# Fused two-part kernel on one core: attention's paired steps joined, transfers planned longer, all orders rewritten

## The chip, the cores and the metric

The kernel runs on one core of one Trainium2 chip. The metric is the device time of one execution in microseconds (us). A core has five engines that matter here, each with its own queue of instructions that it works through strictly in order: TensorE (PE in the profile; PEld is its weight load), VectorE (DVE), ScalarE (ACT), GpSimd (POOL) and SyncE (SP). SP computes nothing; it issues transfers (DMAs) between the core's memory and DRAM. GpSimd issues transfers too.

## What is computed

All data is float32. The first part is a two-way attention for 8 batches and 8 heads, with 512 tokens and 32 state rows of 64 features:

```python
scores = scale * np.matmul(x, state.transpose(0, 1, 3, 2))     # tokens against states
a = np.exp(scores - scores.max(-1, keepdims=True))
a /= a.sum(-1, keepdims=True) + 1e-09
xread = np.matmul(a, state)
scores2 = scale * np.matmul(state, x.transpose(0, 1, 3, 2))    # states against tokens
a2 = np.exp(scores2 - scores2.max(-1, keepdims=True))
a2 /= a2.sum(-1, keepdims=True) + 1e-09
sread = np.matmul(a2, x)
out = np.concatenate([xread, sread], axis=2)
```

The second part takes the 8 x 544 = 4352 rows of 512 features that come out of it through two dense layers of 2048 hidden features:

```python
h = x @ w_in
sp = np.maximum(h, 0.0) + np.log1p(np.exp(-np.abs(h)))   # softplus
g = h * erf(sp)
return g @ w_out
```

## The kernel before

**The algebra.** The product of attention weights, states and `w_in` is regrouped: `mixed` multiplies a batch's states by `w_in` ("M"), and `first_product` multiplies M by the transposed attention weights `aT`, so that `xread` is never formed. The large products are done with seven block products in place of eight (Strassen and Winograd forms; `seven`, `second_product`, and twice over in `twice_product`), which is why there are many additions of blocks on VectorE (`sums_y`, `sums_a`, `sums_w`, the L848 sums of M).

**Stages.** Batch 0 is done in a way of its own during the load of the weights (`begin0`, `mixed0`, `first0`, `serf0`, `second0`). Weights come in through `fetch_in`, `fetch_out` and `fetch_pair` and are rebuilt on ScalarE and VectorE by `convert` (L549 to L557). Then come batches 1 to 7 with the first half of the hidden features (the rounds), each a `unit`: `sums_a`, `second_product` or `twice_product`, with the next batch's `mixed` and `first_product`, and the attention (`attend`) of the batch after that, worked in between. Then the state rows (`first_states`, `second_states`), and then all batches again with the second half of the hidden features.

**The attention of one batch** (`attend`, from L676). Two halves `e` of 512 columns each hold four heads apiece. Per half, in order: four transposes of the x tiles on VectorE (L685; four tiles in all), the scores on TensorE (L693), a copy out of PSUM by ScalarE (L699) into `sc`, then on VectorE a 32 x 32 block transpose into `xT` (L715), the maximum over states (L718), the subtraction (L721), the maximum over tokens (L724) and its scaling (L727), on ScalarE the exponentials (L730 for the token side, L734 for the state side, with the sums accumulated), and on VectorE the sums (L742), the reciprocals (L120 and L121, once for the token side and once for the state side), the scaling (L747), the transpose into `aT` (L752) and the transpose of the state side's weights (L758). Each of the steps stands in a `for e in range(2)` loop, one instruction for each half. At the end `send` writes `xT` to DRAM (`kept_t`, L763) and `receive` reads it back in another layout (L768). `xT` is one buffer for all batches: the next batch's L715 overwrites what L763 reads. The result `sread` is scaled into `sn` by VectorE (L805) in `read`.

**Softplus, erf and the product** (`serf`): ScalarE does softplus (L958) and erf (L973), VectorE the multiplication (L976), then the sums of `sums_a` (L987); TensorE's second product (L1020) reads what these write. Softplus, erf and exp need different function tables, and a change of table is an instruction of its own (ACT_TABLE_LOAD).

**What sets the order.** Every piece of work is recorded by `op(engine, cost, at, go, reads, writes, ...)` with a planned cost. The order on each engine is written out by hand as a list of numbers (`ORDER`, five lists). `emit` walks the five lists with the planned costs, adds a planned cost where ScalarE's table changes, holds transfers back by a planned occupation (`pipe`) and a planned landing (`land`), and emits the instructions in the order of planned begin; `in_order` then pins each engine to that order. So costs set the merge of the engines' lists, but on one engine the order is that of the list. `BY_VECTOR` names the copies out of PSUM that VectorE does; the others go to ScalarE (`either`). `spare_products` are products of an identity matrix that fill waits of TensorE in the first 25 us or so (L115); their results are not used.

Of the kernel before, what the change touches and what calls it, by code (L numbers as in the profile page):

```python
# [11 lines left out]
ALU = mybir.AluOpType  # L12
ACTF = mybir.ActivationFunctionType
AX = mybir.AxisListType
# [3 lines left out]
def kernel(  # L18
# [17 lines left out]
    nc = tc.nc  # L36
# [103 lines left out]
    def op(engine, cost, at, go, reads=(), writes=(), table=None, land=0.0, pipe=0.0):  # L140
# [14 lines left out]
        x0 x2 s00 ta1 m000 m011 m020 m021 m120 m121""".split())  # L155

    def either(name, cost, out, in_, at, reads, writes):

        if name in BY_VECTOR:
            op(DVE, cost[1], at, lambda: nc.vector.tensor_copy(out(), in_()), reads, writes)  # L160
        else:
            op(ACT, cost[0], at, lambda: nc.scalar.copy(out(), in_()), reads, writes)
# [3 lines left out]
            0-1 5 2-3 6 4 8-9 7 15 22-23 17 16 12 24-25 18 10-11 19 13-14 20 26-30 21 34 33 45 31-32  # L166
            54 46 53 47 56 55 71 35 62 37 36 38 48 39-41 70 49 63 57-58 66 74 59-60 43 42 51-52 50
            73 69 44 77-79 61 65 93 81-82 80 83 64 86 84-85 72 76 88-89 94 90 87 95 75 91-92 67 102
            96 68 103 106 97 107 98-99 104 108 130 109 105 132-133 131 137 110 134 111-113 135
            114-115 136 118 140 116 139 138 117 141 119 122-123 143 142 124 100 144 125 101 120-121  # L170
            145 147 126-127 177 128-129 179-180 178 184 181 149-151 182-183 152 186-187 157 153
            158-159 154 160-161 165 188 185 166 189 162-163 167 191 146 155 164 156 148 190 169 168
            170-171 194 192 172 196-198 224 199 173 225-227 174 204 231 228 175 205 229 176 200 234
            206 201 233 230 235 207 202 208 203 232 236 209 237 210-211 238 193 212 195 213-214 239
            241 215 271 243 216 274 217-219 244 273 220 245 272 240 275 221 278 276 242 246 222-223
            281 251-252 277 247 253 248-249 282 280 279 254 250 283 255 284 256-259 286 285 263-265
            260 319 288 287 290 318 291 266 292 261-262 320 293 321 267-268 322 294-295 289 296 325
            269-270 323-324 302 298 328 297 303-306 329 327 326 330 299-301 331 310 307 311 308
            312-313 309 333 332 334 314 364 315 336 316-317 366 365 367 338 337 368 371 343 339 335
            369 344-346 370 340 373-374 347 406 375 372 348-349 376-377 341-342 357 350 359 358 407  # L180
            361 360 352 351 354 353 362-363 356 410-411 355 385 408 387 386 388 378 389 409 390 380
            391 379 382 381 412-413 383-384 414-415 399 392 416-417 393-394 418-419 395 400 396 402
            436 434-435 401 397 403 398 440 420-421 441 437 442-443 404 438-439 444-445 405 446-447
            422-423 449 448 428-429 424 464 425 465 426 432-433 467 427 466 468 430-431 469 471 470
            452 474 454 472 475 455 473 477 476 453 479 478 460 458 450 508 451 456 459 457 509 511
            510 462 461 463 512 487 480 515 489 488 490-491 513 482 481 483 518 492 514 517 484 519
            516 493 485 521 520 501 486 503 494 522-523 496 552 495 502 504 497-498 555 505 499
            553-554 507 506 556 531 500 533 532 559 534-535 524 557-558 525-526 561 528 527 562
            536-537 529 563 560 545 564-565 547 566-567 530 546 538 549 548 539-540 596 542 541 599
            543 550 598 551 603 575 597 544 600 577 568 601 576 578 569 602 579 570 606 572 571 604  # L190
            581 605 607 574 573 580 608-609 582 589 611 610 590-591 640 584 583 585 642 593 592 586
            641 643 595 587 644 619 588 594 645 620-621 612 647 622 614 646 650 623 616 613 615 649
            625 651 648 624 652 617-618 633 653 626 654-655 628 627 635 634 637 636 629-630 684 638
            685 687 686 632 688 639 631 663 689 656 691 657-658 690 693 665 694 664 667 692 666 668
            660 695 659 661 696-697 662 669 699 698 670 677 672 671 729 679 673 678 681 728 674 682
            680 676 731 683 675 707 730 708 710 732 709 700 733 735 711 734 738 702 737 713 739 736
            704 712 701 703 741 705 721 740 706 723 722 714 743 742 725 724 716 715 772 718 774 773
            717 719 775 727 779 776 720 751 726 777-778 753 744 752 754 745 755 746 780 782 748 783
            756 747 784-785 757 749 781 765 750 766 758 768 760 759 767 762 761 769 764 763 770 786
            771 787-790 793 791 795 792 794 797 800 796 802 801 803-804 799 798 807 806 805 809 808  # L200
            814 811 810 816 812 815 818 817 813 819-820""",
        ACT: """
# [1511 lines left out]
```

## Time and profile before

| what | value |
|---|---|
| three runs | 703.06, 703.60, 704.51 us; median 703.6 |
| the profiled execution | 703.79 us, of which the profile's span is 702.0 us |
| granted TensorE clock | 0.999 of full speed |
| busy: PE, PEld, DVE, ACT, POOL | 692.0, 583.9, 593.1, 471.8, 85.6 us |
| moved by DMA | 92.88 MB, mean 132 GB/s |

Times in the trace count from the start of the span. A row of the timeline gives the start, the duration, the engine, the line of the program (L715 is line 715), the operation, what it writes and reads, the shape, the count, and in square brackets the idle time of the engine just before it and what ended that. Instructions of one engine overlap a little at their ends, so the distance between two starts is what a row of instructions really costs. Matmuls are pipelined and their ends are modelled.

### The profile page before, as it was taken

What the parts mean: (1) busy time and instruction counts of PE and PEld (TensorE: products, weight loads), DVE (VectorE), ACT (ScalarE), POOL (GpSimd) and SP (SyncE); (2) the same over time, 40 slices, a digit from 0 to 9 for tenths busy, and PEclk for the clock granted to TensorE, in tenths of its full rate; (3) what the DMA queues carried; (4) which work ended last, traced back from release to release, by engine and by line L of the source; (5) the groups of instructions that cost most, each with busy time, mean ns of one, the idle gap of its engine ahead of it and who ended that gap; (6) DMA issues with size and microseconds to landing.
All of it is one profiled execution on the core that took longest, in us unless ns stands there. A gap on an engine that the chain in (4) does not pass through costs nothing.

```text
span 702.0 us, 13245 instructions
## 1 busy us (share of the span) xinstructions
PE 692.0 (99%) x5193; PEld 583.9 (83%) x5193; DVE 593.1 (84%) x989; ACT 471.8 (67%) x849; POOL 85.6 (12%) x93
## 2 busy tenths in 40 slices
PE   9999999999999999999999999999999999999997
PEld 7534778687878878899999879898989898989997
DVE  6999999899999999896954589686859697869797
ACT  6997997949778475947264665848386748585732
POOL 0001011001010010000100100202043222222231
PEclk9999999999999999999999999999999999999999
DMA  8858896965968655311654502516085536415376
GB/s 284 205 147 201 187 230 168 292 156 174 202 230 189 161 206 188 95 62 30 168 178 180 144 1 83 98 16 114 1 143 68 106 38 114 54 22 70 60 112 116
DMA packets 133742, 92.88 MB, mean 132 GB/s; under 512 B 93744, under 2 KB 120752, under 8 KB 133168
## 3 DMA queue, kind: packets, MB, share of 16 engines
q1 hardware_dynamic: 114336, 61.88, 31.9%
q0 software_dynamic: 18800, 29.63, 23.0%
q8 instruction: 41, 0.67, 0.4%
q10 hardware_dynamic: 544, 0.52, 0.2%
q14 instruction: 21, 0.17, 0.1%
HBM read 50.86 MB, written 41.16 MB: 131 GB/s over the span
## 4 chain that ended last, share of the span: by engine, by line
PE 81%; DVE 9%; ACT 2%; issue 1%; DVEq 0%; ACTq 0%
PE o L1256 30%; PE h L936 17%; PE o L1020 15%; PE at L936 7%; PE o L1439 4%; PE h L1390 2%; PE at L837 2%; PE h L837 2%; PE at L799 1%; DVE ring L976 1%; PE at L1390 1%; DVE ring L987 1%; PE h L693 1%; DVE xT L721 1%; DVE xT L715 1%
## 5 line engine op out<-in xcount | busy, mean ns | idle before, releaser
L948 ACT COPY ring<-h 128x512 f32<-128x512 f32 x120 | 69.1, 584 | 80.4 <-PE h L936 75.0
L976 DVE TENSOR_TENSOR ring<-ring 128x1024 f32<-128x1024 f32 (+1 forms) x64 | 73.0, 1152 | 26.6 <-ACT ring L973 26.2
L936 PE MATMUL h<-aT,m 128*128 128x256 f32 x360 | 92.2, 382 | 0.2 <-ACT ring L948 0.2
L1020 PE MATMUL o<-w_out,ring 128*128 128x256 f32 x320 | 77.7, 382 | 2.2 <-DVE ring L976 2.2
L958 ACT ACTIVATE ring<-ring 128x512 f32<-128x512 f32 x120 | 71.6, 629 | 8.5 <-DVE ring L950 5.5
L936 PEld LDWEIGHTS h<-aT,m 128*128 128x128 f32 x360 | 65.0, 190 | 11.1 <-ACT ring L948 1.1
L987 DVE TENSOR_TENSOR ring<-ring 128x1024 f32<-128x1024 f32 x60 | 72.8, 1220 | 0.4
L1020 PEld LDWEIGHTS o<-w_out,ring 128*128 128x128 f32 x320 | 59.9, 190 | 16.0 <-DVE ring L976 4.2
L1256 PE MATMUL o<-w_out,w_in 128*128 128x128 f32 x512 | 69.8, 276 | 0.0
L1256 PEld LDWEIGHTS o<-w_out,w_in 128*128 128x128 f32 x512 | 65.1, 192 | 3.5 <-issue 0.8
L1256 PE MATMUL o<-w_out,ring 128*128 128x128 f32 x480 | 64.6, 275 | 0.0
L973 ACT ACTIVATE ring<-ring 128x1024 f32<-128x1024 f32 (+1 forms) x64 | 63.4, 1008 | 0.2
L1256 PEld LDWEIGHTS o<-w_out,ring 128*128 128x128 f32 x480 | 60.0, 192 | 1.0 <-DVE ring L1281 0.2
L1020 PE MATMUL o<-raw,ring 128*128 128x256 f32 x240 | 58.6, 381 | 0.0
L1020 PEld LDWEIGHTS o<-raw,ring 128*128 128x128 f32 x240 | 44.9, 190 | 8.3 <-issue 1.7
L1256 PE MATMUL o<-raw,ring 128*128 128x128 f32 x360 | 48.7, 276 | 0.0
L1256 PEld LDWEIGHTS o<-raw,ring 128*128 128x128 f32 x360 | 45.3, 192 | 1.6 <-DVE xT L1238 0.8
L1176 POOL DMA_DIRECT2D out_dram<-oo x16 | 23.3, 1487 | 168.6 <-DVE ring L976 71.5
L1256 PE MATMUL o<-raw,xT 128*128 128x128 f32 x320 | 41.2, 276 | 0.1
L1256 PEld LDWEIGHTS o<-raw,xT 128*128 128x128 f32 x320 | 38.8, 192 | 2.6 <-ACT o L1287 0.8
L936 PE MATMUL h<-sy,m 128*128 128x256 f32 x120 | 30.9, 380 | 0.1
L936 PE MATMUL at<-sy,sx 128*128 128x256 f32 x120 | 31.0, 381 | 0.0
(269 smaller groups left out, 1400.5 us busy)
## 6 DMA issues: line engine op xcount, KB each, us to landing
x<-in_x_dram SPq DMA_DIRECT2D x30, 256.0 KB, 5.2
xq<-in_x_dram SPq DMA_DIRECT2D x112, 64.0 KB, 2.6
out_dram<-oo SPq DMA_DIRECT2D x10, 512.0 KB, 4.6
raw<-in_moe_w_in_dram SPq DMA_DIRECT2D x8, 512.0 KB, 6.9
raw<-in_moe_w_out_dram SPq DMA_DIRECT2D x4, 1024.0 KB, 5.7
raw<-in_moe_w_in_dram POOLq DMA_DIRECT2D x8, 512.0 KB, 5.7
raw<-in_moe_w_out_dram POOLq DMA_DIRECT2D x8, 512.0 KB, 5.6
kept_a<-aT SPq DMA_DIRECT2D x8, 512.0 KB, 4.2
```

The costliest lines, as they stand in the source:

```text
L837: nc.tensor.matmul(out=bank(names[k])[Ns * p:Ns * p + Ns, :], lhsT=st[r, b, q], rhs=of_group[2 * u + j][r, :, i, :], start=True, stop=True)
L936: nc.tensor.matmul(out=out_[:, i], lhsT=x_[:, q:q + P], rhs=y_, start=(start and i == 0), stop=(i == 1), skip_group_check=not start)
L948: op(ACT, 0.5, t, lambda: nc.scalar.copy(out_(), view(bank(name))), [name], w)
L958: op(ACT, 0.53, t, lambda: nc.scalar.activation(out=part(splane, k), in_=part(hplane, k), func=ACTF.Softplus), area(hplane, ks=[k], os=[o] ...
L973: op(ACT, 0.085 + 0.875 * share, at + n, lambda s_=s_: nc.scalar.activation(out=s_, in_=s_, func=ACTF.Erf), [], area(splane, ks=[k], os=os ...
L976: op(DVE, 0.065 + 1.075 * share, at + n + 1, lambda s_=s_, h_=h_: tt(s_, s_, h_, op=ALU.mult), area(hplane, ks=[k], os=os), area(splane, k ...
L987: op(DVE, 1.14, at + k, lambda k=k, x_=x_, y_=y_, how=how: tt(get("h", k), get(*x_), get(*y_), op=how), area(v[x_[0]], ks=[x_[1]]) + area( ...
L1020: nc.tensor.matmul(out=view(name)[:, h], lhsT=lhs[:, i, :], rhs=weight_of[n]()[:, u, i, :], start=(start and h == 0 and i == 0), stop=(h = ...
L1176: op(GP, 1.2, t, lambda: nc.gpsimd.dma_start(out=quad(r, c), in_=one(v), accum_op=ALU.add), every(*v), [("out", b, r, c)], land=3.0, pipe=2.0)
L1256: nc.tensor.matmul(out=out_[:, Q2 * k:Q2 * k + Q2], lhsT=lhs[:, k, i], rhs=rhs[:, i], start=first, stop=(k == len(ns) - 1 and i == 1), ski ...
L1390: nc.tensor.matmul(out=bank(bk)[:, P * i:P * i + P], lhsT=x_[:, i, k], rhs=y_[:, k], start=(start and i == 0 and k == 0), stop=(i == GF - ...
L1439: nc.tensor.matmul(out=bank("o%d" % bk)[:, E2 * c:E2 * c + E2], lhsT=ring[:, w_[w], plane, k][:, i, :], rhs=weight_of[n]()[:, u, i, :], st ...
```

## The change

1. In `attend`, the loops over the two halves become single instructions over 1024 columns: the transposes L715, L752 and L758, the maxima L718 and L724, the subtraction L721, the exponentials L730, the sums L742 and the scaling L747. The x transposes L685 go from four to two, except for batch 1, whose tiles arrive one by one. The two reciprocals (token and state side) become one, on one buffer `z`. The state side's exponential L734 stays in two.
2. The scaling into `sn` may now be done by ScalarE: `either` gets a `by` argument, and 5 of the 14 stay with VectorE. `BY_VECTOR` is rewritten, so other copies of batch 0's stage change engine.
3. Planned costs: a table load 1.28 becomes 1.41; occupations of transfers grow (x 5.2 to 6.0, `keep_y` 2.7 to 3.0, `put` 1.5 to 1.7, the late weight fetches 1.7 to 2.0, `kept_in` 0.9 to 1.2, batch 0's output 0.8 to 1.0).
4. All five lists of `ORDER` are new.

```diff
     BY_VECTOR = set("""
-        x0 x2 s00 ta1 m000 m011 m020 m021 m120 m121""".split())
+        x1 st s01 ta0 ta1 z1 m020 m021 u0 u1 m120 m121 sn11 sn40 sn41 sn51 sn70""".split())
...
+            if by:
+                nc.vector.tensor_scalar(out(), in_(), by(), None, op0=ALU.mult)
...
+            if by:
+                nc.scalar.activation(out=out(), in_=in_(), func=ACTF.Copy, scale=by())
...
-                cost, loaded[ACT] = cost + 1.28, table
+                cost, loaded[ACT] = cost + 1.41, table
...
-            op(SP, 3.0, 60, lambda: load_x_static(1), [], ["x"], land=4.0, pipe=5.2)
+            op(SP, 3.0, 60, lambda: load_x_static(1), [], ["x"], land=4.0, pipe=6.0)
...
-        for e in range(2):
-            dve(0.62, lambda e=e: nc.vector.transpose(out=both()[:, e], in_=sc()[:, e]),
-                [sc_of(b, e)], ["xT%d" % e])
-        for e in range(2):
-            dve(0.6, lambda e=e: nc.vector.reduce_max(out=m1()[:, e], in_=a(e), axis=AX.X),
-                ["xT%d" % e], ["m1%d" % e])
...
+        dve(1.19, lambda: nc.vector.transpose(out=flat(both()[:, 0:2]), in_=flat(sc())), scs, xts)
+        dve(1.136, lambda: nc.vector.reduce_max(out=m1(), in_=a(), axis=AX.X), xts, ["m1"])
+        dve(1.135, lambda: tt(a(), a(), over(m1()), op=ALU.subtract), ["m1"], xts)
+        dve(1.136, lambda: nc.vector.reduce_max(out=m2(), in_=sc(), axis=AX.X), scs, ["m2"])
...
+        op(ACT, 0.96, at + 6, lambda: nc.scalar.activation(
+            out=a(), in_=a(), func=ACTF.Exp, scale=scale), [], xts, table="exp")
...
-        dve(0.72, lambda: (inverse(z1()), inverse(z2())), [],
+        dve(0.37, lambda: inverse(z()), [],
...
-            op(DVE, 0.2, at + 1, lambda e=e: nc.vector.tensor_scalar(
-                sn_tile(b)[:, e], bank("at1")[:, D * e:D * e + D], d["z2"]()[:, e:e + 1], None,
-                op0=ALU.mult), ["at1", "z2%d%d" % (b % 2, e)], ["sn%d%d" % (b % 2, e)])
+            either("sn%d%d" % (b, e), (0.25, 0.2), lambda e=e: sn_tile(b)[:, e],
+                   lambda e=e: bank("at1")[:, D * e:D * e + D], at + 1,
+                   ["at1", "z2%d%d" % (b % 2, e)], ["sn%d%d" % (b % 2, e)],
+                   by=lambda e=e: d["z2"]()[:, e:e + 1])
```

The built program shows what the new lists do. VectorE has 900 instructions in place of 989, ScalarE 833 in place of 835, with 51 table loads in place of 53; TensorE has the same work, spare products included. On SP, in the list before, two pairs of `kept_a` and `kept_y` (`keep_y`) directly follow the third store of `xT` (L763); in the new list none stands between the third and the fourth store: batch 0's pair comes earlier, ahead of the x tiles of batch 2, and batch 3's after the fourth store. On VectorE, the work between the transpose L758 of one batch and the transpose L715 of the next is different in each round.

More of the change, by code (lines that the diff above doesn't have):

```diff
@@ L159, in either @@
         if name in BY_VECTOR:
[L160 removed]
+            op(DVE, cost[1], at, vector, reads, writes)
         else:
[L162 removed]
+            op(ACT, cost[0], at, scalar, reads, writes)
     ORDER = {
         PE: """
[L166 to L167 removed]
@@ L168 @@
[L168 to L173, printed above, removed]
```

306 lines of the change are left out of this document (151 added, 155 removed), and 4 rows, old and new, of the table ORDER.

## Prediction

> **What bounds the kernel now.** I read the page first.
>
> ```profile
> span 702.0 us, 13245 instructions
> PE 692.0 (99%) x5193; PEld 583.9 (83%) x5193; DVE 593.1 (84%) x989; ACT 471.8 (67%) x849; POOL 85.6 (12%) x93
> ```
>
> TensorE is busy for 692.0 of 702.0 us, and the change takes no matrix product away. So nothing that VectorE or ScalarE saves counts by itself; only TensorE's idle time can shrink, 10.0 us in all. The view of busy time by stretches says where it lies.
>
> ```profile
> 0.00:10.00 10.00, 8.94 (x115) 7.62 (x116) 3.45 (x6) 4.28 (x7) 0.69 (x6) 1.00 0.82 267
> 10.00:20.00 10.00, 9.16 (x101) 7.96 (x99) 9.60 (x21) 8.44 (x15) 0.00 (x0) 1.00 0.95 296
> 20.00:30.00 10.00, 9.82 (x49) 4.88 (x48) 9.93 (x15) 9.91 (x14) 0.00 (x0) 1.00 0.67 138
> 30.00:40.00 10.00, 9.57 (x42) 4.05 (x41) 9.15 (x14) 9.31 (x13) 0.00 (x0) 1.00 1.05 295
> 40.00:50.00 10.00, 9.85 (x51) 3.58 (x50) 9.72 (x15) 9.90 (x12) 0.00 (x0) 1.00 0.34 110
> 50.00:60.00 10.00, 9.94 (x29) 4.51 (x29) 9.97 (x17) 8.55 (x14) 0.93 (x2) 1.00 0.61 99
> 130.00:140.00 10.00, 8.66 (x40) 7.02 (x38) 7.29 (x14) 9.97 (x16) 0.01 (x1) 1.00 1.05 347
> 140.00:160.00 20.00, 19.06 (x87) 16.49 (x88) 19.93 (x29) 9.98 (x19) 2.89 (x5) 1.00 0.69 162
> 160.00:320.00 160.00, 160.00 (x1196) 132.22 (x1195) 151.29 (x262) 112.76 (x188) 6.86 (x12) 1.00 0.58 163
> 360.00:600.00 240.00, 240.00 (x1804) 215.60 (x1804) 180.44 (x293) 155.51 (x297) 39.18 (x34) 1.00 0.42 84
> 600.00:702.00 102.00, 97.25 (x772) 91.74 (x770) 83.93 (x142) 54.66 (x119) 23.00 (x20) 0.99 0.48 73
> ```
>
> The first figure after each stretch is its length; then come the busy times of TensorE, its weight loads, VectorE, ScalarE and GpSimd, the granted clock, the DMA engines' busy share and GB/s. Three places hold the idle time: the first 60 us (1.06 + 0.84 + 0.18 + 0.43 + 0.15 + 0.06 = 2.72), 130 to 160 us (1.34 + 0.94 = 2.28), and the end (4.75, the last results on their way out, which the change leaves as they are). From 160 to 320 and from 360 to 600 us there is none: savings there are worth nothing. In the first 60 us more is hidden, because spare products fill waits:
>
> ```profile
> L115 PE MATMUL o<-ident 128*128 128x128 f32 x64 | 8.4, 280 | 0.1
> ```
>
> These 8.4 us are no work, so an earlier start of real work could gain up to their length too. The waits of TensorE name one large one:
>
> ```profile
> PE o L1020 <- DVE ring L976: 2.2, 1, 2.2
> ```
>
> I looked at its neighbourhood in the timeline.
>
> ```profile
> 130.73 0.71 DVE L758 STREAM_TRANSPOSE xT<-xT 128x512 f32<-128x512 f32 x1
> 131.47 0.34 SPq L763 DMA_DIRECT2D kept_t<-xT  x1
> ...
> 135.67 0.68 DVE L1034 TENSOR_TENSOR oo<-oo,o 128x512 f32<-128x512 f32 x1
> ...
> 138.33 0.64 ACT L549 ACTIVATE m<-raw 128x512 f32<-128x512 f32 x1
> 138.88 1.04 ACT L973 ACTIVATE ring<-ring 128x1024 f32<-128x1024 f32 x1
> 139.02 0.71 DVE L715 STREAM_TRANSPOSE xT<-m 128x512 f32<-128x512 f32 x1 [2.67 <-ACT m L549]
> 139.66 1.18 DVE L976 TENSOR_TENSOR ring<-ring 128x1024 f32<-128x1024 f32 x1
> ...
> 140.89 1.35 PE L1020 MATMUL o<-w_out,ring 128*128 128x256 f32 x5 [2.24 <-DVE ring L976]
> ```
>
> VectorE stands still for 2.67 us before L715, and L976, which TensorE needs, is queued behind it. The profile names ScalarE's L549 as what ended the wait, but L715 reads nothing of it; L715 writes `xT`, and `xT` is being read by the store `kept_t`, issued at 131.47. The view of transfers, for 120 to 142 us, for the whole run, and for the stores of batches 1 and 2 alone, in this order:
>
> ```profile
> kept_t<-xT SPq DMA_DIRECT2D x1, 512.0 KB, 7.5
> ...
> kept_t<-xT SPq DMA_DIRECT2D x7, 512.0 KB, 3.6
> ...
> kept_t<-xT SPq DMA_DIRECT2D x1, 512.0 KB, 3.6
> ...
> kept_t<-xT SPq DMA_DIRECT2D x1, 512.0 KB, 2.9
> ```
>
> 131.47 + 7.5 = 138.97, and L715 starts at 139.02. The store took 7.5 us, twice its median of 3.6, because the DMA engines were full (share 1.05 from 130 to 140 us). So **the one wait that a plan can remove is a transfer's landing**, and it costs TensorE 2.24 us.
>
> **The change part by part.** *The joined steps.* What one wide instruction saves over two halves, by the distance of starts:
>
> ```profile
> 56.86 1.22 DVE L131 TENSOR_TENSOR raw<-w_out 128x1024 f32<-128x1024 f32 x1
> 58.00 1.29 DVE L721 TENSOR_TENSOR xT<-xT,m 128x512 f32<-128x512 f32 x2
> 59.20 0.42 DVE L874 TENSOR_TENSOR aT<-aT 128x256 f32<-128x256 f32 x1
> ...
> 85.77 0.10 DVE L120 TENSOR_SCALAR z<-z 128x2 f32<-128x2 f32 x1
> ...
> 85.99 0.67 DVE L747 TENSOR_TENSOR xT<-xT,z 128x512 f32<-128x512 f32 x1
> ```
>
> A 1024-wide one takes 58.00 - 56.86 = 1.14, two halves 59.20 - 58.00 = 1.20: 0.06 saved. Five such pairs (L718, L721, L724, L742, L747) make 0.30. No 1024-wide transpose is in the trace; it lies between 1.14 and two halves, so five pairs of transposes save 0 to 0.3 in a batch; I take 0.15, the middle, since the two ends are close. The second reciprocal with its addition goes: 85.99 - 85.77 = 0.22. About 0.67 us per attention and 4.7 for seven, on VectorE. ScalarE saves one start of L730 per batch, which no row shows; between 0 and twice VectorE's 0.06, so at most 0.8 in seven batches. On the path: nothing from 160 us on, where TensorE never idles. Ahead of 160 us it is part of the queue sums below. If TensorE's cover were gone there, it would be these 4.7 us that come back.
>
> The Trainium skill's page "Perfetto Trace Analysis", section "Optimizing Scalar/DVE Operations", speaks against this part: where ScalarE and VectorE aren't saturated but cause bubbles on other engines, breaking up instructions may let work complete sooner. VectorE is at 9.15 to 9.97 of 10 us from 10 to 60 us, which is the page's other case, where grouping helps; at 130 to 140 us it is at 7.29, which is the case it warns of. What joining could cost there is a rival below.
>
> *`sn` moved to ScalarE and fewer table loads.*
>
> ```profile
> L805 DVE TENSOR_SCALAR sn<-at,z 128x64 f32<-128x64 f32 x14 | 3.6, 273 | 0.7 <-PE at L799 0.6
> L973 ACT ACT_TABLE_LOAD x17 | 21.8, 1283 | 0.3
> ```
>
> Nine of 14 scalings leave VectorE, 9 x 0.27 = 2.4 at most; No row shows that form on ScalarE; I bound one by 0 and by the 0.64 of L549, and take VectorE's 0.27, 2.4 us in all. Two of 53 table loads go, 2 x 1.28 = 2.6 us of ScalarE. ScalarE is busy for 67% of the span; after the first stage both are hidden by TensorE's own work and I cost them at 0.
>
> *The first 60 us.* Here VectorE and ScalarE are both full, and the order decides.
>
> ```profile
> 14.65 0.68 DVE L462 TENSOR_REDUCE m1b<-at 128x16 f32<-128x512 f32 x1
> ...
> 20.78 3.60 PE L605 MATMUL h<-aT,m 128*128 128x512 f32 x8
> ...
> 23.37 1.28 ACT L612 ACT_TABLE_LOAD   x1
> ...
> 52.30 1.28 ACT L617 ACT_TABLE_LOAD   x1
> ...
> 55.08 0.68 DVE L621 TENSOR_TENSOR ring<-ring,at 128x512 f32<-128x512 f32 x1
> ...
> 69.02 0.65 DVE L848 TENSOR_TENSOR sx<-m 128x512 f32<-128x512 f32 x1
> ```
>
> I added up, for the old and the new order, the durations of all instructions that stand on an engine ahead of such a point. In the new order the maximum of batch 0's second half (14.65) stands ahead of three pieces of weight conversion and copies, about 2 us earlier in VectorE's queue; one more copy into `aT` goes to VectorE (+0.6), so L605 may start up to 1 us before 20.78. ScalarE reaches its first softplus table (23.37) no earlier (+0.3), but its last erf table of the stage (52.30) 1.1 us earlier, since copies went to VectorE. VectorE in turn reaches the product at 55.08 0.4 to 1.0 later, and the sums of batch 1's M (69.02) 2.7 earlier. TensorE needs both engines. The gain lies between -1.0 (VectorE's delay alone) and 2.7 (VectorE's lead at 69.02, which is also all the idle time outside the spare products). I take **0.7**, between ScalarE's 1.1 and nothing, because ScalarE's row is the nearest to what TensorE waits for between 20 and 55 us.
>
> *The transfers.* In the old order 4.9 us of VectorE's work, ten pieces, stand between L758 and the next L715 at the wait (131.44 to 136.35, where the row at 135.67 ends). In the new order there stand four sums L848, one L874, two L976 and two L987 of full width, the joined L724 with its scaling, an L553 and an L950: 5 of 0.6 (half a pair of 1.20), 5 of 1.14 and three small ones of 0.7 together: 3.0 + 5.7 + 0.7 = 9.4 us. That is more than the 7.5 us the store took, and the two `keep_y` pairs that followed the store on SP are no longer behind it. So L715 does not wait there: **2.2 us** of TensorE come back (the 2.24). What is late next is ScalarE, busy 9.97 of 10 us in that stretch; its fourth L973 ends at 139.92, but the new order has the first L976 about 9 us of VectorE's work earlier in its queue, so I count the whole.
>
> *Sum*, against the profiled execution: 703.79 us, of which 702.0 is the span and 1.8 lies around it. 702.0 - 2.2 - 0.7 = 699.1, and with 1.8 around it 700.9. The median of the three runs is 0.2 below the profiled one, so I predict **700.7**.
>
> **The rivals.** *(A) More comes back in the first stage.* If TensorE hangs on VectorE throughout the first 60 us, the 2.7 of the row at 69.02 count in place of 0.7: 698.7. For it: VectorE is at 9.72 and 9.97 of 10 us from 40 to 60 us. Against it: TensorE's idle time between 20 and 60 us is only 0.82.
>
> *(B) The wait is replaced by another.* L715 no longer waits, but TensorE then waits for ScalarE, full at 9.97 in that stretch: only the first stage's 0.7 is gained, 702.9. For it: the full ScalarE. Against it: the new order has ScalarE's erf of that round further ahead too.
>
> *(C) Joined halves make each attention's chain longer.* The exponential of the first half now waits for the second half's subtraction, and the sums for both exponentials, 0.6 and 0.5 us, 1.1 a round; if two rounds have no other work in between, TensorE loses 2 x 1.1 and the kernel takes 702.9. It is the page's case above. Against it: between subtraction and sums the new order has an L131 of 1.14 us in the first round.
>
> *(D) Slower: the landing of `kept_t` stalls the two earlier rounds.* The new order leaves less work between L758 and the next L715 there: 4.9 us after batch 1's store and 4.3 after batch 2's. In the old trace these stores landed in 3.6 and 2.9 us, which fits. But the new lists put other transfers beside them; with the 7.5 us of the third store, VectorE would wait 2.6 + 3.2 = 5.8 us, and TensorE 2.24/2.67 of it, 4.9. Less the 2.9 gained, 2.0 slower: 705.6 on the scale of the median. It decides from where both landings reach about (4.9 + 4.3 + 2.9 x 2.67/2.24)/2 = 6.3 us.
>
> *(E) The change doesn't do what it says*: the built order shows the joined instructions, so only the new plan could miss, which is B and D.
>
> **How the numbers follow.** About 0.2% (1.4 us) is what a measurement of this kernel can tell from no change: faster is below 702.2, slower above 705.0. Forecast 0.48 (its own range 699.5 to 702.0), A 0.12, B 0.13, C 0.09, D 0.18. Faster: the forecast, A, and little of B, 0.61. Slower: D without its mild cases, 0.16. The same: the rest of B, C and D, 0.23. The range reaches from A less half a us to D: 698.2 to 705.8.
>
> **What would show it.** Right: no idle time of VectorE above 1 us before the joined L715 of batches 2, 3 and 4; TensorE's wait of 2.24 gone from 130 to 160 us; L605 starting at 20 or a little earlier; VectorE's busy time about 5 to 7 us down with TensorE's unchanged. Wrong: an L715 that starts just when `kept_t` lands, now after batch 1 or 2 (D); a wait of TensorE for ScalarE's L973 around 130 us (B); idle time on TensorE between 20 and 60 us that grows (then the first stage's sign was wrong); or new waits after 160 us, where I see no cause for any.

## The result, and the profile after

The changed kernel takes 699.12 us (median of 4 runs, 698.86 to 699.40) against 703.33 us before (4 runs, 702.86 to 704.51): a ratio of 0.9947 with a 95% interval of 0.9931 to 0.9962. The prediction said 700.7, with 699.5 to 702.0 as the forecast's own range. The profiled execution took 699.40 us, 697.6 of it the span, against 703.79 and 702.0. The page of the changed kernel:

```profile
span 697.6 us, 13137 instructions
...
PE 690.2 (99%) x5193; PEld 583.9 (84%) x5193; DVE 586.3 (84%) x900; ACT 467.3 (67%) x847; POOL 85.9 (12%) x93
```

VectorE has 6.8 us less to do and TensorE 1.8 (its products are the same; at least part of what fell is time in which started products waited for operands, as in the score products below). The stretches of the first 20 us and of the old wait, with the columns as before:

```profile
0.00:10.00 10.00, 9.03 (x88) 7.77 (x88) 3.05 (x6) 3.75 (x6) 0.69 (x6) 1.00 0.83 267
10.00:20.00 10.00, 9.43 (x128) 8.40 (x128) 9.29 (x20) 8.55 (x16) 0.00 (x0) 1.00 0.88 282
130.00:140.00 10.00, 10.00 (x71) 7.67 (x55) 9.93 (x15) 7.76 (x13) 1.30 (x2) 1.00 1.00 281
140.00:160.00 20.00, 20.00 (x93) 17.38 (x92) 19.23 (x26) 14.53 (x26) 1.29 (x2) 1.00 0.55 126
```

From 130 to 160 us TensorE no longer stands still (2.28 us before). The wait on L976 (now L977) is not among its waits any more; the largest that are left:

```profile
PE o L115 <- PEq L1699: 0.8, 1, 0.8
PE o L446 <- ACT xT L169: 0.5, 1, 0.5
PE o L1257 <- DVE ring L1282: 0.3, 1, 0.3
PE o L456 <- DVE ring L481: 0.3, 1, 0.3
```

The timeline around the third store, and the store's landing (the line of the view of transfers for 135 to 139 us):

```profile
134.78 1.23 DVE L758 STREAM_TRANSPOSE xT<-xT 128x1024 f32<-128x1024 f32 x1
135.94 0.64 DVE L849 TENSOR_TENSOR sx<-m 128x512 f32<-128x512 f32 x1
136.03 0.34 SPq L763 DMA_DIRECT2D kept_t<-xT  x1
...
138.89 1.22 DVE L977 TENSOR_TENSOR ring<-ring 128x1024 f32<-128x1024 f32 x1
...
145.81 1.24 DVE L732 STREAM_TRANSPOSE xT<-m 128x1024 f32<-128x1024 f32 x1
```

```profile
kept_t<-xT SPq DMA_DIRECT2D x1, 512.0 KB, 3.6
```

Two things are to be seen. The next transpose into `xT` (L732) has 9.8 us of other work before it and no idle time. And the store lands in 3.6 us, not 7.5, so even the old gap of 4.9 us would have done. The prediction did not count on the second. The DMA engines are as busy as before in this stretch (share 1.00 against 1.05 from 130 to 140 us), so being full alone, the prediction's reason for the 7.5 us, does not stretch the landing.

To see where the time went, I took three points at which TensorE has done the same products in both orders: the first L605 (after: L614), the first L936 (L937) after 60 us, and an L1020 (L1021) near 169 us. The table gives their distances in the traces of all kernels of this study, in us; the experiments follow below.

| kernel | span's start to first L605 | to L936 near 66 | to L1020 near 169 | to the end of the span |
|---|---|---|---|---|
| before | 20.78 | 45.35 | 102.58 | 533.29 |
| costs_only (old orders) | 21.70 | 45.07 | 102.23 | 533.30 |
| kin_early (old orders, one move) | 21.59 | 44.89 | 101.11 | 533.31 |
| keep_moved (old orders, one move) | 21.62 | 45.32 | 101.35 | 537.11 |
| turn_later (old orders, one move) | 21.66 | 45.20 | 100.26 | 533.58 |
| two_moves (old orders) | 20.78 | 45.30 | 100.28 | 533.24 |
| three_moves (old orders) | 21.57 | 45.25 | 101.34 | 533.24 |
| joined_before (old orders) | 21.06 | 45.14 | 101.80 | 535.90 |
| after | 20.71 | 44.93 | 98.92 | 533.04 |
| halves_back (new orders) | 20.34 | 44.58 | 99.23 | 533.15 |
| both_back (new orders, moves) | 20.05 | 44.94 | 99.45 | 533.06 |
| copies_back (new orders) | 20.24 | 44.87 | 98.97 | 533.02 |
| sn_vector (new orders) | 20.62 | 44.92 | 100.84 | 533.02 |
| tail_split (new orders) | 20.38 | 44.91 | 98.90 | 533.11 |

Between the two profiled executions the 4.4 us are 0.07 + 0.42 up to 66 us, 3.66 from there to 169 us, and 0.25 after it. The table also shows what one pair of executions hides: the first column of the old orders goes from 20.78 to 21.70, and the execution that the prediction was made from was one of the earliest.

The runs say the same. In later runs on three chips the kernel before took 703.20, 702.37 and 702.71 us in the median, but single runs lay between 700.8 and 707.9. The new orders are far steadier: 698.85 to 699.53 in halves_back and 698.74 to 699.62 in tail_split, six runs each.

### The profile page after: what moved, and what is told of

It reads as the page before. It is cut to its first block, busy times and chain, and to the rows that moved or that the text cites. A ratio compares the mean times of both kernels' runs of the same rounds, so it can differ in the third digit from the quotient of the medians.

```text
span 697.6 us, 13137 instructions
## 1 busy us (share of the span) xinstructions
PE 690.2 (99%) x5193; PEld 583.9 (84%) x5193; DVE 586.3 (84%) x900; ACT 467.3 (67%) x847; POOL 85.9 (12%) x93
## 4 chain that ended last, share of the span: by engine, by line
PE 89%; DVE 4%; ACT 1%; issue 0%; DVEq 0%
PE o L1257 29%; PE h L937 19%; PE o L1021 18%; PE at L937 7%; PE o L1440 4%; PE o L639 2%; PE h L1391 2%; PE at L838 2%; PE h L838 2%; PE at L799 1%; PE h L706 1%; PE at L1391 1%; DVE ring L977 1%; PE at L614 1%; DVE ring L988 0%
## 5 line engine op out<-in xcount | busy, mean ns | idle before, releaser
L977 DVE TENSOR_TENSOR ring<-ring 128x1024 f32<-128x1024 f32 (+1 forms) x64 | 73.3, 1153 | 23.9 <-ACT ring L974 23.9
L937 PE MATMUL h<-aT,m 128*128 128x256 f32 x360 | 91.6, 381 | 0.2 <-ACT m L844 0.2
L1021 PE MATMUL o<-w_out,ring 128*128 128x256 f32 x320 | 77.7, 382 | 0.0
L937 PEld LDWEIGHTS h<-aT,m 128*128 128x128 f32 x360 | 65.5, 190 | 10.1 <-issue 1.3
L1021 PEld LDWEIGHTS o<-w_out,ring 128*128 128x128 f32 x320 | 59.6, 190 | 11.9 <-DVE m L566 1.7
L1021 PE MATMUL o<-raw,ring 128*128 128x256 f32 x240 | 59.8, 380 | 0.0
L1021 PEld LDWEIGHTS o<-raw,ring 128*128 128x128 f32 x240 | 45.2, 190 | 8.6 <-issue 2.5
L1177 POOL DMA_DIRECT2D out_dram<-oo x16 | 25.9, 1736 | 164.5 <-DVE m L1239 77.8
L1177 POOL DMA_DIRECT2D out_dram<-m x15 | 22.1, 1624 | 104.9 <-ACT ring L959 38.2
L937 PE MATMUL h<-sy,sx 128*128 128x256 f32 x120 | 31.2, 382 | 0.0
```

What stands on the lines that cost most here:

```text
L937: nc.tensor.matmul(out=out_[:, i], lhsT=x_[:, q:q + P], rhs=y_, start=(start and i == 0), stop=(i == 1), skip_group_check=not start)
L977: op(DVE, 0.065 + 1.075 * share, at + n + 1, lambda s_=s_, h_=h_: tt(s_, s_, h_, op=ALU.mult), area(hplane, ks=[k], os=os), area(splane, k ...
L1021: nc.tensor.matmul(out=view(name)[:, h], lhsT=lhs[:, i, :], rhs=weight_of[n]()[:, u, i, :], start=(start and h == 0 and i == 0), stop=(h = ...
L1177: op(GP, 1.2, t, lambda: nc.gpsimd.dma_start(out=quad(r, c), in_=one(v), accum_op=ALU.add), every(*v), [("out", b, r, c)], land=3.0, pipe=2.0)
```

## The experiments

The theory behind the prediction was that the new orders carry the gain, above all by taking away the wait behind the third `kept_t` store, and that the joined steps are worth next to nothing on the path. The rival was that the joined steps carry it.

**halves_back: the changed kernel without the joining.** The other joined steps are edited like these two:

```diff
-        dve(1.136, lambda: nc.vector.reduce_max(out=m1(), in_=a(), axis=AX.X), xts, ["m1"])
+        dve(1.136, lambda: halves(lambda e: nc.vector.reduce_max(
+            out=part(m1(), e), in_=part(a(), e), axis=AX.X)), xts, ["m1"])
...
-        dve(0.37, lambda: inverse(z()), [],
+        dve(0.37, lambda: (inverse(z1()), inverse(z2())), [],
```

> The changed kernel with every joined step of attention issued as two instructions of 512 columns again, one directly after the other, and the two reciprocals apart; lists, transfers and everything else as changed. Theory O (the new orders carry the gain, because what they took away is a wait of 2.24 us behind the landing of the third kept_t store and small stalls beside it): VectorE's busy time rises by 4 to 6 us, which TensorE's work hides from 160 us on, and the time rises by at most 0.8 us, to 699.1 to 699.9. Rival J (the joined steps carry it, by what VectorE saves): the 4.2 us come back, about 703.3.

Measured: 699.13 us (6 runs), ratio to the kernel before 0.9939 (0.9917 to 0.9960). The changed kernel has 699.12 and 0.9947. The engines' busy time in its page:

```profile
PE 690.0 (99%) x5193; PEld 583.8 (84%) x5193; DVE 589.5 (85%) x982; ACT 467.9 (67%) x854; POOL 85.9 (12%) x93
```

VectorE does 3.2 us more and TensorE nothing. In the new orders the joining is worth nothing that can be measured; rival J falls.

**joined_before: the kernel before with the joining alone.** Of two halves, one entry of the list issues the wide instruction and the other nothing:

```diff
+        def second(step, wide):
+            if (step in done) != (step == "t"):
+                wide()
+            done.add(step)
...
-            dve(0.6, lambda e=e: tt(a(e), a(e), over(m1()[:, e]), op=ALU.subtract),
+            dve(0.6, lambda e=e: second("s", lambda: tt(aw(), aw(), wide(m1()), op=ALU.subtract)),
```

> The kernel before with the joined steps alone: its five lists stay, each joined instruction stands where the later of its two halves stood (the transpose into xT where the earlier stood), the x transposes L685 stay in four. Theory O: the wait behind the third kept_t store stays (2 to 3 us of VectorE), and the time stays within 0.8 us of the kernel before, 702.5 to 704.1. Rival J: 4 us faster, about 699.3. Rival C of the prediction (joined halves lengthen the chain): up to 2.2 slower, 705.5.

Measured: 706.57 us (10 runs), ratio 1.0049 (1.0033 to 1.0064): 3.4 us slower. VectorE saves 4 us of work, and TensorE pays in new waits. In its timeline three matmuls with idle time before them, each with the joined piece that delayed it:

```profile
78.99 1.06 ACT L743 ACTIVATE xT<-xT 128x1024 f32<-128x1024 f32 x1 [0.88 <-DVE xT L734]
...
83.00 1.13 PE L951 MATMUL h<-aT,m 128*128 128x256 f32 x4 [0.78 <-ACT ring L963]
...
175.96 1.24 DVE L726 STREAM_TRANSPOSE xT<-sc 128x1024 f32<-128x1024 f32 x1
...
177.83 1.13 PE L1035 MATMUL o<-w_out,ring 128*128 128x256 f32 x4 [0.68 <-DVE oo L1049]
...
270.73 1.21 DVE L755 TENSOR_REDUCE z<-xT 128x32 f32<-128x1024 f32 x1
...
272.60 1.13 PE L951 MATMUL at<-aT,sx 128*128 128x256 f32 x4 [0.55 <-DVE ring L965]
```

(Lines are 11 to 15 further down here: L743 is the joined exponential L730, L726 the joined L715, L755 the joined sums L742; L951 is L936, L1035 is L1020, L963 is L948.) ScalarE stands still for the joined subtraction, with the copies that TensorE needs (L963) queued behind. On VectorE small additions for TensorE stand directly behind the wide pieces: L1049 at 177.12 behind L726, L965 at 271.86 behind L755. The first of the three is rival C's mechanism, the longer chain; the other two are another one, small pieces that TensorE needs queued behind wide ones. Together joining without a new order costs 1.5 times what rival C had. The expected wait behind the third store did not stay: the store landed in 3.8 us here, and TensorE's wait on its L991 (L976 before) is 0.3 us.

**turn_later: only the waiting transpose moved.** VectorE's list of the kernel before, entry 245 being the first half's L715 of batch 4:

```diff
-221 245 226 220 251 153 228 269 252 229 244 227
+221 226 220 251 153 228 269 252 229 245 244 227
```

> The kernel before with one entry of VectorE's list moved: the first half's transpose L715 of batch 4, which waited for the landing of the kept_t store, now stands directly ahead of the second half's, 5.6 us of VectorE's work later. Nothing else is changed. Theory O: VectorE's idle 2.67 us and TensorE's 2.24 us go, 703.3 - 2.2 = 701.1 (700.7 to 701.6). Rival B of the prediction (ScalarE's erf is late next): no change, 702.9 to 703.3.

Measured: 702.79 us (12 runs), ratio 0.9997 (0.9981 to 1.0013). The trace does what was expected: the store takes 6.4 us, but L976 no longer stands behind it (it started at 139.66 before).

```profile
132.19 0.34 SPq L763 DMA_DIRECT2D kept_t<-xT  x1
137.00 1.22 DVE L976 TENSOR_TENSOR ring<-ring 128x1024 f32<-128x1024 f32 x1
```

The stretch to 169 us falls from 102.58 to 100.26. The median doesn't fall with it, against the 701.1 expected. The next run shows why a single profile is no measure of this wait.

**costs_only: the same program with the new planned costs.** The edit, besides the longer occupations:

```diff
-                cost, loaded[ACT] = cost + 1.28, table
+                cost, loaded[ACT] = cost + 1.41, table
```

> The kernel before with all planned costs of the change (a table load 1.41, the longer occupations of transfers) and its own five lists: each engine then gets the same instructions in the same order. Theory: the planned costs act through the lists alone, so the time is that of the kernel before, 703.2 within 0.5, with the same spread of several us from run to run. Rival: they act by themselves, over 1 us faster. Its profile is also a second look at the old orders: if the wait of TensorE behind the third kept_t store is a matter of the landing, it will be there with another length (the landing between 5 and 8 us, TensorE's wait between 0 and 2.5).

Measured: 702.64 us (10 runs), ratio 1.0003 (0.9993 to 1.0014), 701.37 to 704.07. Planned costs do nothing but shape the lists. As a second execution of the old orders it has the same wait, shorter (landing 7.1), and here the profile names the releaser that it misnamed before:

```profile
139.31 0.71 DVE L715 STREAM_TRANSPOSE xT<-m 128x512 f32<-128x512 f32 x1 [2.31 <-DMA kept_t<-xT]
139.95 1.18 DVE L976 TENSOR_TENSOR ring<-ring 128x1024 f32<-128x1024 f32 x1
141.19 1.13 PE L1020 MATMUL o<-w_out,ring 128*128 128x256 f32 x4 [1.86 <-DVE ring L976]
```

**keep_moved: the `keep_y` pairs away from the store.** SP's list of the kernel before; 36 is the store, 46 and 39 the pairs, 43 the x tiles:

```diff
-36 46 41 39 40 43 37
+36 41 40 43 46 39 37
```

> The kernel before with two entries of SP's list moved: the two keep_y pairs that followed the third kept_t store stand behind the load of the next x tiles (L710 in the changed kernel's numbering of xq). VectorE's list is unchanged, so the gap between L758 and L715 stays at 4.9 us. Theory O in the form that the prediction gave it (the pairs right behind the store stretch its landing to 7.5 us): the store lands in 3.6 to 5 us, the wait goes, 701.1. Rival (other traffic of that stretch, the weight fetches on the other queue above all, sets the 7.5): landing 6 us or more, the wait stays at least 1 us, 702.2 to 703.3.

Measured: 703.35 us (12 runs), ratio 1.0006 (0.9988 to 1.0025). The first line is from the view of transfers for 126 to 145 us, the others from the waits:

```profile
kept_t<-xT SPq DMA_DIRECT2D x1, 512.0 KB, 6.2
```

```profile
PE at L1390 <- DVE ring L1406: 2.0, 1, 2.0
...
PE o L1020 <- DVE ring L976: 1.0, 1, 1.0
```

The landing stays over 6 us without the pairs, as the rival had it, so they are not what stretches it. The 2.0 us at L1390, near 364 us, are new and belong to a second weak place of the old orders:

```profile
DVE aT L1357 <- DMA xq<-kept_in: 8.3, 1, 8.3
```

In the profile of the kernel before VectorE waits there too, 6.0 us, for a load of `kept_in` issued at 353.43 that landed in 7.8; TensorE just had enough work. Here the load took 8.7 us, and it had not. The changed kernel issues that load at 344.55, and the wait is gone.

**kin_early and two_moves.** SP's list of the kernel before, 79 and 78 being the loads of `kept_in`; two_moves has this edit and that of turn_later:

```diff
-73 81 78 75 79 74 80
+73 79 78 81 75 74 80
```

> The kernel before with two entries of SP's list moved: the loads of kept_in into xq and x stand right behind the first outputs of batch 6's second stage and ahead of the reload of batch 1's weights, as in the changed kernel. Theory L (the old orders hang on landings at two places, the third kept_t store and, near 360 us, the load of kept_in, where VectorE waited 5.3 to 8.3 us and TensorE lost 3.8 us in one profile and nothing in three): VectorE's wait at L1357 is gone, the slow runs of 704 to 707 us go, the median falls by 0.3 to 1. Rival (that loss had another cause): the spread stays.

Measured: 702.68 us (12 runs, 700.71 to 705.06), ratio 1.0002 (0.9991 to 1.0014). The wait at L1357 is gone from the trace, but the median doesn't fall by the 0.3 to 1 expected, and two runs over 704 us remain. The first wait is there again, smaller still:

```profile
137.91 0.71 DVE L715 STREAM_TRANSPOSE xT<-m 128x512 f32<-128x512 f32 x1 [1.20 <-ACT ring L948]
...
139.78 2.43 PE L1020 MATMUL o<-w_out,ring 128*128 128x256 f32 x10 [0.75 <-DVE ring L976]
```

> The kernel before with both moves: L715 of batch 4 later on VectorE, and the loads of kept_in earlier on SP. Theory L: neither landing is waited for any more; the time is 701 (700.5 to 702), and the runs lie within 1.5 us of one another. Rival J (joined steps) and every theory in which the landings are not the cause: 702.8 to 703.2 with the old spread.

Measured: 701.94 us (11 runs), ratio 0.9987 (0.9977 to 0.9996), and 701.24 to 702.84 where the kernel before had 700.81 to 705.06 on the same chip. Here the spread behaves nearly as theory L said (1.6 us), but three_moves below, which contains both moves, lies between 701.66 and 704.17, so a narrower spread is not shown. The median falls by 0.3 to 1.6 us, less than the 2.2. The old orders' wait was 2.24, 1.86, 0.98 (keep_moved) and 0.75 us in four executions with the same VectorE list. Its cost is a matter of the execution, and in the median no more than about 1.6.

**both_back: the old surroundings put back into the changed kernel.** VectorE's list (211 is the joined L732 of batch 4), then SP's:

```diff
-224 200 201 214 215 136 202 199 228 211 212
+224 200 201 211 214 215 136 202 199 228 212
...
-33 39 38 36 43 41 37 40 44 46 50
+33 38 36 46 39 43 41 37 40 44 50
```

> The changed kernel with the third store's old surroundings: the two keep_y pairs stand right behind it on SP again, and the joined transpose L732 of batch 4 stands five pieces, about 5 us, behind L758 instead of 9.8. Theory L: VectorE waits 1 to 2.5 us for the landing, TensorE 0.8 to 2.2, so 700 to 701.3, with more spread. Rival (the changed order has other work ready at that point, so a landing costs nothing there): 699.1 to 699.4.

Measured: 700.02 us (5 runs, 699.32 to 700.32), 0.9 more than the changed kernel. But the reason is not the expected one:

```profile
135.40 0.34 SPq L763 DMA_DIRECT2D kept_t<-xT  x1
...
140.65 1.24 DVE L732 STREAM_TRANSPOSE xT<-m 128x1024 f32<-128x1024 f32 x1
...
146.44 1.13 PE L937 MATMUL at<-aT,sx 128*128 128x256 f32 x4 [0.45 <-DVE ring L951]
```

L732 doesn't wait: the store landed in 3.7 us, with both pairs next behind it on SP's queue (the first `kept_a` was issued at 135.79). The loss seen is that L732 now stands ahead of L951, which TensorE needs; it costs TensorE 0.45 us in this trace, half of the 0.9. Without the pairs the landing stayed long (keep_moved), with them it is short here: they don't decide it. What stands on SP's queue ahead of the store differs too. In the changed kernel:

```profile
125.16 5.99 SPq L784 DMA_DIRECT2D x<-in_x_dram  x4
```

The four x loads are issued until 131.15, 4.9 us before the store at 136.03. In the kernel before the same row is 123.97 and 5.98, so they are issued until 129.95, 1.5 us before the store. All fourteen traces fall into two groups by that distance (us from the end of the issuing to the store, then the store's landing): 1.2 and 6.7, 1.5 and 7.5, 1.7 and 6.4, 2.1 and 7.1, 2.2 and 6.2, 2.8 and 5.3, 3.1 and 6.0; then 4.1 and 3.8, 4.4 and 4.4, 4.8 and 3.8, 4.9 and 3.6, 5.0 and 3.6, 5.2 and 3.7, 7.4 and 3.5. So a store that closely follows 1 MB of x lands late. That is a correlation: the long landings are all of old orders, the short ones of the new orders and joined_before, and no run moves the x loads alone. Waiting behind x can't be all of it either. In kin_early the last x load, issued at 127.86, landed at 131.9, just as the store was issued (131.82), and the store still took 6.0 us. What was on its way then came from GpSimd's queue, a weight fetch and a store of `kept_in`, issued from 129.08 on. The first line is from the view of transfers for 127.85 to 128.70 us, the others from that for 128.90 to 132 us:

```profile
x<-in_x_dram SPq DMA_DIRECT2D x1, 256.0 KB, 4.0
```

```profile
raw<-in_moe_w_in_dram POOLq DMA_DIRECT2D x1, 512.0 KB, 5.5
kept_t<-xT SPq DMA_DIRECT2D x1, 512.0 KB, 6.0
kept_in<-m POOLq DMA_DIRECT2D x1, 256.0 KB, 5.5
```

The Trainium skill's page "DMA: Bandwidth & Descriptors", section "Queues, rings and completion order", says that each DMA engine consumes the descriptors of a ring in order; the row of pairs agrees with that, the trace of kin_early is not explained by it. The rival of keep_moved, traffic from the other queue, stays open.

**three_moves: what is left between 66 and 169 us.** two_moves with VectorE's x transposes of batches 2 and 3 (110 109 107 108 and 194 193 192 191) earlier:

```diff
-73 91 93 75 110 109 107 108
+73 110 109 107 108 91 93 75
...
-136 137 143 194 193 192 191
+194 193 192 191 136 137 143
```

> The kernel before with the two moves of the run above and, on VectorE, the four x transposes L685 of batch 2 and of batch 3 each moved 3 to 3 pieces (1.3 and 1.8 us) earlier, ahead of the work that stood before them. Theory S (what is left between the old and the changed orders from 66 to 169 us, 1.36 us, is small waits of TensorE, 0.44 of it in score products L693 that take the x tiles as each is transposed): the two stretched sets of score products (1.29 to 1.31 us each) become 1.02, the stretch from the first L936 after 66 us to the L1020 at 169 us shrinks from 100.28 to about 99.8, the time to 701.5. Rival: what was moved behind them (the sums of aT, the weight conversion) is late instead, 701.9 or more.

Measured: 703.15 us (12 runs), ratio 1.0001 (0.9984 to 1.0017). Of the two sets of score products one became shorter (1.30 before), one not:

```profile
69.60 1.09 PE L693 MATMUL o<-xq,st 64*32 64x512 f32 x16
95.03 1.29 PE L693 MATMUL h<-xq,st 64*32 64x512 f32 x16
```

The stretch to 169 us grew from 100.28 to 101.34, because pieces behind the moved ones came late (waits of TensorE of 0.2 to 0.3 us on L948 and L906 from 103 to 114 us). The rival is right: these single moves don't bring what the new lists bring.

**copies_back: which engine sets the first stage.**

```diff
-            op(DVE, cost[1], at, vector, reads, writes)
+            op(DVE, cost[1], at, scalar if name in ("ta0", "z1", "u0", "u1") else vector,
+               reads, writes)
```

> The changed kernel with four copies out of PSUM of the first stage done by ScalarE again, where the change gave them to VectorE: one into aT, one of the state rows z, and the two of the turned states; they stand at the same places of the order. Theory of the prediction (ScalarE's lead of 1.1 us is what the first stage gains): ScalarE is up to 1.8 us later, the L639 near 52 and 59 us start 0.5 to 1.1 later, the time is 699.6 to 700.2. Rival (VectorE decides, rival A): VectorE is freed of 2 us, the time stays or falls, 698.6 to 699.2.

Measured: 698.62 us (6 runs, 698.21 to 698.99). ScalarE is late once, as expected, but TensorE makes it up by 47 us:

```profile
PE o L640 <- ACT st L169: 0.9, 1, 0.9
```

So ScalarE's lead is not what the first stage gains. That VectorE is the engine to spare there, as the rival says, fits but is not shown: the stage ends at 65.11 us here and between 64.92 and 65.64 in the other new orders, and while the median is 0.6 us under tail_split, which ran on the same chip and has the changed kernel's time, the two ranges overlap.

**sn_vector: the scalings back on VectorE.**

```diff
-            op(ACT, cost[0], at, scalar, reads, writes)
+            op(ACT, cost[0], at, vector if by else scalar, reads, writes)
```

> The changed kernel with the nine scalings into sn that ScalarE got done by VectorE again, at the same places of the order. Prediction's term: 0, so 699.0 to 699.4. Rival (the sn products gate the next read on TensorE): 0.3 to 1 slower.

Measured: 700.79 us (10 runs), ratio 0.9970 (0.9958 to 0.9982): 1.6 us over tail_split on the same chip, the rival at more than its price. The place, in this kernel:

```profile
162.61 1.20 DVE L755 STREAM_TRANSPOSE aT<-xT 128x1024 f32<-128x1024 f32 x1
...
163.74 0.24 DVE L161 TENSOR_SCALAR sn<-at,z 128x64 f32<-128x64 f32 x1
163.90 1.23 DVE L758 STREAM_TRANSPOSE xT<-xT 128x1024 f32<-128x1024 f32 x1
...
165.06 0.24 DVE L161 TENSOR_SCALAR sn<-at,z 128x64 f32<-128x64 f32 x1
...
165.35 0.33 PE L813 MATMUL at<-ident,sn 128*128 128x128 f32 x1 [1.20 <-DVE sn L161]
```

and in the changed kernel:

```profile
162.75 0.52 ACT L167 ACTIVATE sn<-at,z 128x64 f32<-128x64 f32 x2
...
163.59 0.27 PE L813 MATMUL at<-ident,sn 128*128 128x128 f32 x1
```

A piece of 0.24 us behind two joined transposes costs TensorE 1.20. A list made for `sn` on VectorE would place it better; what is shown is that the wide instructions and the move of `sn` belong together.

**tail_split: the last transfers from two queues.**

```diff
+                on = nc.scalar if cols.start else nc.sync
-                op(SP, 0.4, at + 26, lambda h=h, cols=cols: nc.sync.dma_start(
+                op(SP, 0.4, at + 26, lambda h=h, cols=cols, on=on: on.dma_start(
```

> The changed kernel with the last of the three final output transfers, which SP issues one after the other, issued by ScalarE, which is idle by then. Theory (the last half us of the span is SP's issuing): the last transfer starts up to 0.5 us earlier, 698.6 to 699.1. Rival (the landing of the last result alone sets the end): 699.1, no change. A second look at the changed orders as well.

Measured: 699.19 us (6 runs), no change. The two last transfers now start together,

```profile
693.31 0.37 ACTq L1307 DMA_DIRECT2D out_dram<-ring  x1
693.49 0.60 SPq L1307 DMA_DIRECT2D out_dram<-ring  x1
```

and their landing takes what the issuing saved: 2.7 us for the 128 KB one where it took 2.4.

## Why the prediction was right, and where it wasn't

*As a whole.* The way was right: 4.2 us faster where 2.9 were forecast. But 699.12 lies below the forecast's own range and nearer to rival A's 698.7 than to 700.7, and what A gave as the reason, 2.7 us in the first stage, didn't come. Where the gain lies on the scale of the medians can be put together from the table and the waits: 1.3 us up to 66 us, 1.4 in small waits after it, 0.2 after 169 us, and the wait behind the store with about the 1.5 that it had in the mean of four executions (2.24, 1.86, 0.98, 0.75). That makes 4.4, an estimate, against 4.2 measured. So the term of 2.2 was too large, that of 0.7 too small, and 1.6 us were in no term; that the errors partly cancel is luck.

*The joined steps, costed at 0 on the path.* Right: 699.13 without them. The sizes were near: VectorE's busy time rises by 3.2 us when they are taken apart (4.7 worked out), and a 1024-wide transpose takes 1.24, 1.16 from start to start (134.78 to 135.94), close to the lower end of the bounds.

*Rival C, and the page "Perfetto Trace Analysis" of the Trainium skill beside it.* Not what happened here, but real: in the old order joining alone costs 3.4 us. That rule of the Trainium skill, that breaking up instructions may help where VectorE isn't full but causes bubbles, agrees with the traces there: joined_before waits at 177.83 and 272.60 us for VectorE, which is busy for 146.3 of the 160 us from 160 to 320. New lists are what makes the joining free. The prediction saw the place wrongly too: it looked at 130 to 140 us, and the loss lay mostly after 169 us (535.90 against 533.3), where it had called all changes worth nothing because TensorE never idles.

*`sn` on ScalarE, costed at 0.* Wrong. The rows priced it nearly right (ScalarE takes 0.31 each; 0.27 was taken), but "hidden by TensorE's own work" failed: TensorE waits on the small piece itself, and with wide instructions ahead of it on VectorE that is 1.6 us.

*The first 60 us, 0.7.* The sum was too small and its reason was wrong. In the profiled pair it is 0.5. In the means of the table, the old orders reach L605 at 21.36 and L936 at 66.54 (six traces whose lists agree up to there), the new ones at 20.42 and 65.28 (five, without copies_back): 0.94 to L605 and 0.32 from there, 1.26 in all. "L605 up to 1 us earlier" was the right step, and my profile couldn't show it, since it began 0.6 us earlier than the mean. In the old orders the time of L605 follows the time of the second x tile's transposes L411 (5.45 to 6.38 us); in the new ones they start between 5.37 and 6.23 and L614 starts between 20.05 and 20.71 all the same. The wait that shrinks is on VectorE's L472, 1.0 us in two_moves and 0.3 (L481) in the changed kernel:

```profile
PE o L447 <- DVE ring L472: 1.0, 2, 0.6
```

That fits the earlier maximum in VectorE's new order; no run here tests it by itself. ScalarE's 1.1 us, from which I took the 0.7, are not the cause (copies_back).

*The transfers, 2.2.* The step is right in the profiled pair: the wait of 2.24 is gone, L732 has 9.8 us of work ahead of it (9.4 worked out), and turn_later takes the same wait away with one move. Two things were off. The size was that of one execution (0.75 to 2.24). And of the two reasons given, "the pairs are no longer behind it" is refuted by keep_moved and both_back; why the landing is short is open (the x loads are further ahead of the store, but kin_early shows that this is not all). Either the gap or the landing would have been enough.

*What the sum lacked.* From 66 to 169 us the new orders take 98.9 us where the old ones take 100.3 with the big wait removed, 1.4 us in small waits of 0.2 to 0.4 each (in two_moves at 69, 82, 94 and 155 us). I read only the large wait of that stretch, and left out the score products stretched to 1.30 us and the waits on L948. A further 0.2 comes after 169 us. So the profiled pair gained 4.4 where 2.9 was predicted: 1.4 of the difference lies here.

*The rivals.* D didn't come: the two earlier stores landed in 3.9 and 2.8 us. The prediction's sign of no idle time above 1 us at the joined transposes failed at one (L732 of batch 2, 1.5 us), but that wait is for the score copies and costs TensorE nothing. B didn't: ScalarE is at 7.76 of 10 us from 130 to 140, not 9.97. A may have the right engine (copies_back), and the first stage gave about half of its 2.7. "New waits after 160 us, where I see no cause for any" holds for the changed kernel, but the old orders had a near miss there that I passed over because TensorE didn't pay for it in that one execution.

*What stays open.* The profiles put the old wait at 0.75 to 2.24 us, and two_moves gains 0.3 to 1.6 in the median; whether unprofiled executions wait less was not measured. What stretches the store's landing is not shown: ring order behind x and traffic from GpSimd's queue are both left. The 1.4 us of small waits are located, not taken apart: three_moves, the one trial, made them worse in its one trace.

## What to carry to other kernels

On an engine that works in order, a step's price is what stands behind it: joining instructions cost 3.4 us, nothing, or made a 0.24 us piece cost 1.2, by the list alone. A wait that ends with a transfer is to be read from several executions, and in two places: the work between issue and wait, and what else is on its way when the transfer is issued, on its own queue and on others. A stall that TensorE doesn't pay for in one profile may be paid for in another run.

## What the hardware showed that was not expected

In keep_moved the stall near 364 us cost more than itself. The stretches around it, with the granted clock in the column after the five engines:

```profile
363.00:365.00 2.00, 0.13 (x1) 0.13 (x1) 2.00 (x3) 0.15 (x1) 0.83 (x1) 0.97 0.00 2
365.00:367.00 2.00, 2.00 (x10) 2.00 (x11) 1.88 (x3) 1.98 (x3) 0.34 (x1) 0.50 0.61 53
367.00:369.00 2.00, 2.00 (x14) 2.00 (x14) 0.51 (x1) 1.71 (x4) 0.00 (x0) 0.68 0.50 78
369.00:371.00 2.00, 2.00 (x20) 2.00 (x20) 2.00 (x4) 0.64 (x2) 0.00 (x0) 1.00 0.00 0
```

After 2.0 us without work TensorE ran at half its clock for about 3.4 us, and 2.0 us of waiting became 3.8 (537.11 against 533.3 in the table). After the 2.24 us at 139 us in the kernel before, the clock stayed at 1.00. The Trainium skill's page "TensorE: Matmul & The Clock Gate", section "What's actually happening", states that the clock is halved after an idle window of about 3.4 us; here 2.0 us were enough once, and 2.24 were not another time. Of 148 runs of the kernel before and of its versions with moved entries or new planned costs, 11 took over 705 us; 8 of these show a mean clock of 0.996 or 0.997, and one of the other 137 does. That fits such a stall in them, but only this one was seen in a profile.
